# Geglu after sliding-window attention: a third seven-product quad in the last two token groups

## The chip, the cores and the metric

The kernel runs on one core of one Trainium2 chip. The metric is the device time of one execution in microseconds (us), taken as the median of several runs. TensorE does matrix products and writes them to PSUM banks, VectorE (DVE) and ScalarE (ACT) read the banks, GpSimd (POOL) works on data in on-chip memory, and SyncE (SP) issues transfers. Each engine runs its own instructions in their order; semaphores tie the engines together.

## The reference: attention, then a gated feed-forward block

For 8 batches, 8 heads, 576 positions and 64 columns a head:

```
scores = q @ k.T / 8 + slope[h] * -|i - j|        (kept where 0 <= i - j < 128)
attn   = softmax(scores) @ v
x      = attn, heads side by side                  # 4608 tokens x 512
out    = (gelu(x @ w_gate) * (x @ w_val)) @ w_out  # 512 -> 1536 -> 512
```

Inputs and the output are f32. The kernel computes the products in bf16 with f32 sums.

## The kernel before: nine token groups, quads and plain blocks

The 4608 tokens go through the feed-forward block in nine groups of 512 (g = 0 to 8). Attention of later batches runs between the groups and is finished in group 6; **groups 7 and 8 have feed-forward work alone**. The 1536 hidden columns are twelve blocks f of 128. `hid[g]` (hT in the trace) holds a group's hidden values, blocks by tokens.

Blocks are made in two ways.

A **plain block** (`gate_val`, L631) takes 8 matmuls of 512 tokens: 4 into a bank for the gate, 4 into a bank for the value. ScalarE takes the gelu of the gate (L655), VectorE multiplies (L656).

A **quad** (`gate_quad`, L811) makes four blocks at once, in a Strassen-like way: the tokens are cut in a low and a high half of 256, the inner dimension in two halves, and gate and value are the two columns of the small matrix. Seven products take the place of eight. They run in the order 1, 2, 6, 5, 7, 3, 4; each has 8 matmuls of 256 tokens, two halves u = 0 and 1 of four matmuls, each half in its own bank. Products 1, 6, 7 and 4 go into bank x of their half, 5 and 3 into y, 2 into z. So a later product accumulates on what an engine has read out in between: ScalarE copies product 1 (L849), then 1 + 6 (L855), and product 5 (L858) into three pairs of f32 staging tiles; VectorE adds banks to these (L839); ScalarE takes the gelus (L842); VectorE multiplies the low half of the tokens out of bank x (L872), GpSimd the high half out of staging (L876). In groups 6 to 8 the staging tiles are buffers of the attention part that lie idle by then (`rooms`, L805): qT0 for product 1, kT0 for 1 + 6, qT1 for product 5, and qs0 for the gelus, the same for every quad.

Products 3, 5, 6 and 7 need four sums of weights (`combine_weights`, eight instructions: four sums for two 128-row pieces), made once for a quad's place. Those for blocks 6 to 9 are in `kept`; those for blocks 0 to 3 are made by GpSimd into the tile P0 at the end of group 6. Products 4 to 7 need four sums of inputs, made by `combine_x` for each group (by VectorE for group 8, during the products of group 7).

The table `QUADS = (0, 6)` sets the order in groups 7 and 8: quad on blocks 0 to 3, plain blocks 4 and 5, quad on 6 to 9, plain blocks 10 and 11.

The **output** of groups 2 to 8 uses the same scheme (`product`, L741): the left operand is hT, split by block parity and token half; three sums of it go to `left` and one is made in place in hT (`combine_left`, L718, in four steps s1, s2, in-place a21, s4). Blocks pair up as i = 0 to 5 (blocks 2i and 2i + 1). Each product n has 6 matmuls of 256 columns for each of a = 0 and 1; groups 7 and 8 run n = 1, 2, 6, 5, 7, then 3 and 4 (group 8 begins 4 after one matmul of 3). Products 1 and 2 read the low token half of hT, 6 left sum s2, 5 s1, 7 the in-place sum, 3 s4, and 4 the high half of hT. `gather_out` names what is read out of the banks: p1, u2, p5 and c21 are copies by ScalarE, c11, c22 and c12 additions by VectorE (L902, L908, L913).

Everything is in a hand-written order: the engines execute what the program issues in its order, and nothing is rescheduled. Eight PSUM banks are shared by all of this.

Of the kernel before, what the change touches and what calls it, by code (L numbers as in the profile page):

```python
# [25 lines left out]
QUADS = (0, 6)  # L26
# [10 lines left out]
def kernel(  # L37
# [680 lines left out]
    def combine_left(g, lo, hi, which=(0, 1, 2, 3), engine=nc.vector):  # L718
        x, ns = halves(g), slice(lo, hi)
# [21 lines left out]
    def product(g, n, a, lo=0, hi=NF // 2):  # L741
        (l, r), into = FACTORS[n], INTO[n]
        first = n in (1, 2, 5)
# [4 lines left out]
        for i in range(lo, hi):  # L748
            lhsT = left[:, l, i, cols] if isinstance(l, int) else halves(g)[:, i, l[0], l[1], cols]
            rhs = right[:, r, i, :] if isinstance(r, int) else x[:, i, r[0], r[1], :]  # L750
            nc.tensor.matmul(out=made[g, a, into], lhsT=lhsT, rhs=rhs, start=first and i == 0,  # L751
                             stop=i == NF // 2 - 1, skip_group_check=True)

    def flat_of(t):
# [3 lines left out]
    sums_w = {0: [flat_of(Ps[0])[:, 1024 * n:1024 * n + 1024].rearrange("p (c f) -> p c f", c=2) for n in range(4)],  # L758
              6: [kept[:, n, :, :] for n in range(4)]}

    def combine_weights(f0, engine=nc.gpsimd):
        todo, to = [], sums_w[f0]
        for c in (0, 1):
            g1, g2, v1, v2 = (w[:, x, 128 * f0:128 * f0 + 512]
                              for w, x in ((wg, c), (wg, 2 + c), (wv, c), (wv, 2 + c)))
            s1, s2, s3, s4 = (t[:, c, :] for t in to)
# [44 lines left out]
    def gate_quad(g, f0, room=None, between=None):  # L811
# [6 lines left out]
        g1, g2, v1, v2 = (w[:, c:c + 2, 128 * f0:128 * f0 + 512] for w in (wg, wv) for c in (0, 2))  # L818
# [3 lines left out]
        def P(n):  # L822
            w, x = factors[n]
            for u in (0, 1):
# [3 lines left out]
                for e in (0, 1):  # L828
                    at = 256 * u + 128 * e
                    for c in (0, 1):  # L830
                        nc.tensor.matmul(  # L831
                            out=ps[:, 256 * e:256 * e + 256], lhsT=w[:, c, at:at + 128], rhs=x[:, c, :],
                            start=n in (1, 2, 5) and e == 0 and c == 0, stop=c == 1, skip_group_check=True)
# [10 lines left out]
        def hidden(u, half):  # L844
            return hid[g][:, f0 + 2 * u:f0 + 2 * u + 2, 256 * half:256 * half + 256]
# [24 lines left out]
        P(4)  # L870
        for u in (0, 1):
            nc.vector.tensor_tensor(out=hidden(u, 0), in0=cut(banks["x", u], 2), in1=cut(gelu_tiles[u], 2), op=ALU.mult)  # L872
            n = P5[u].shape[1]
            out, high = hidden(u, 1), cut(gelu_tiles[2 + u], n)
            if n == 2:
                nc.gpsimd.tensor_tensor(out=out, in0=P5[u], in1=high, op=ALU.mult)  # L876
            else:
                nc.gpsimd.tensor_tensor(
                    out=out.rearrange("p e (y x) -> p e y x", x=128),
                    in0=P5[u].rearrange("p (e y) x -> p e y x", e=2),  # L880
                    in1=high.rearrange("p (e y) x -> p e y x", e=2), op=ALU.mult)
# [268 lines left out]
    def out_products(g):  # L1150
# [3 lines left out]
        if b > B:  # L1154
            last = [(4, ("c21",)), (3, ("c12",))]
            for n, after in [(1, ("p1",)), (2, ()), (6, ("u2", "c11")), (5, ("p5",)), (7, ("c22",))] + (
                    last if g == NG - 1 else last[::-1]):
                early = g == NG - 1 and n in (3, 4)
                for a in (0, 1):
                    if early and a == 0 and n == 4:  # L1160
                        P(3, 0, 0, 1)
                    P(n, a, *((1,) if early and a == 0 and n == 3 else ()))
# [3 lines left out]
                if n == 6 and g + 1 < NG:  # L1166
                    combine_x(g + 1)
# [73 lines left out]
        P(3, 0, 0, 2)  # L1241
        P(4, 0)
        P(3, 0, 2)
# [39 lines left out]
    for g in range(NG):  # L1283
        if 1 <= g < B - 2:
            transposes_dma(3 if g == 1 else g + 2)
        if g >= B - 1:
            for f in range(NF):
                if f in QUADS:
                    gate_quad(g, f)
                elif not any(f0 < f < f0 + 4 for f0 in QUADS):  # L1290
                    gate_val(g, f)
                if f == 4:
                    store()
                if f == 5:
# [116 lines left out]
```

## Time and profile before

| | us |
|---|---|
| median of 3 runs (lowest to highest) | 326.07 (326.05 to 326.29) |
| the profiled execution | 324.97 |
| its span, from the first to the last instruction | 323.2 |
| group 7 from its first gate matmul to the first of group 8 (263.06 to 291.39) | 28.33 |
| group 8 to its last output matmul but the tail (291.39 to 319.72) | 28.33 |

A row of the timeline gives the start, the time of all instructions in the row, engine, line, operation, output <- inputs, shapes and count; what stands in brackets is the engine's idle time before it and what ended it. Where one row has several instructions, they overlap a little, so the start of the next is a better measure of their pace than their length. A matmul's length holds its way through the array; its pace is read from starts.

### The profile page before, as it was taken

The page shows a single profiled execution, that of the slowest core. Times are in us where ns is not written, and L with a number is a line of the kernel's source. Part 1 is how long each engine was busy: PE and PEld are TensorE (multiplying, and loading weights), DVE is VectorE, ACT ScalarE, POOL GpSimd, SP SyncE. Part 2 cuts the span into 40 slices and gives each one's busy share as a digit, 9 for nine tenths or more (in the row PEclk, how much of TensorE's full clock was granted, in tenths as well). Part 3 has the DMA queues.
Part 4 walks back from the last instruction along what each step waited for, and adds up shares of the span by engine and source line. Part 5 has one row for each costly group of instructions (what it writes and reads, how often), then busy time and mean ns, then how long its engine had stood idle before and what let it go on. Part 6 is the DMA issues. An engine that isn't in the chain of part 4 may idle for free.

```text
span 323.2 us, 9412 instructions
## 1 busy us (share of the span) xinstructions
PE 316.2 (98%) x3753; PEld 213.8 (66%) x3753; DVE 248.6 (77%) x493; ACT 219.5 (68%) x421; POOL 196.9 (61%) x228
## 2 busy tenths in 40 slices
PE   8999999999999999999989999999999999999995
PEld 4566746565554767566855786578747787788764
DVE  7789666979779877967697679877897756895692
ACT  7984678557888678657956787578767256627641
POOL 5973679385069986379936995496009496410450
PEclk9999999999999999999999999999999999999999
DMA  8999999999999979976997699759204230003003
GB/s 217 165 195 192 200 176 178 142 168 192 124 154 175 140 148 193 171 138 160 173 195 140 173 164 191 138 159 146 101 35 100 51 132 0 2 0 132 0 4 130
DMA packets 149920, 43.57 MB, mean 135 GB/s; under 512 B 133588, under 2 KB 142964, under 8 KB 149876
## 3 DMA queue, kind: packets, MB, share of 16 engines
q0 software_dynamic: 107456, 18.10, 75.6%
q1 hardware_dynamic: 41424, 23.35, 33.5%
q10 hardware_dynamic: 996, 1.53, 1.9%
q8 instruction: 29, 0.48, 0.6%
q14 instruction: 15, 0.12, 0.1%
HBM read 43.65 MB, written 9.53 MB: 165 GB/s over the span
## 4 chain that ended last, share of the span: by engine, by line
PE 91%; DMA 4%; ACT 2%; DVE 1%; issue 1%; DVEq 0%; ACTq 0%
PE ps L648 35%; PE ps L751 20%; PE ps L831 19%; PE ps L497 5%; PE ps L685 4%; DMA wo<-in_moe_w_out_dram 4%; PE ps L307 2%; PE ps L221 1%; ACT P L236 1%; PE ps L78 1%; PE ps L435 1%; PE ps L705 1%; PE ps L1001 1%; PE ps L345 1%; DVE T L391 0%
## 5 line engine op out<-in xcount | busy, mean ns | idle before, releaser
L648 PE MATMUL ps<-xT,wg 128*128 128x512 bf16 (+4 forms) x312 | 71.9, 352 | 0.0
L648 PE MATMUL ps<-xT,wv 128*128 128x512 bf16 (+4 forms) x312 | 71.8, 352 | 0.0
L655 ACT ACTIVATE gelu<-ps 128x512 bf16<-128x512 f32 (+3 forms) x77 | 41.6, 546 | 41.4 <-PE ps L648 37.6
L656 DVE TENSOR_TENSOR hT<-ps,gelu 128x512 bf16<-128x512 f32 (+3 forms) x77 | 46.3, 623 | 19.2 <-PE ps L648 15.4
L236 ACT ACTIVATE P<-ps 128x512 bf16<-128x512 f32 (+1 forms) x108 | 52.3, 578 | 5.6 <-PE ps L307 3.0
L648 PEld LDWEIGHTS <-wv 128*128 128x128 bf16 x312 | 29.2, 98 | 30.4 <-DVE xT L556 0.8
L648 PEld LDWEIGHTS <-wg 128*128 128x128 bf16 x312 | 28.7, 98 | 26.1 <-issue 0.3
L241 DVE TENSOR_TENSOR P<-P,emask 128x768 bf16<-128x768 bf16 x60 | 31.8, 551 | 7.7 <-ACT P L236 6.0
L751 PEld LDWEIGHTS <-hT 128*128 128x128 bf16 x336 | 32.1, 98 | 6.6 <-issue 0.8
L117 POOL DMA_DIRECT2D vb<-in_v_dram x40 | 34.0, 886 | 3.6 <-DMA wo<-in_moe_w_out_dram 1.0
L876 POOL TENSOR_TENSOR hT<-qT,qs 128x512 bf16<-128x512 f32 x10 | 11.5, 1166 | 26.5 <-ACT qs L842 26.5
L117 POOL DMA_DIRECT2D ks<-in_k_dram x30 | 25.4, 890 | 2.9 <-DMA qs<-in_q_dram 2.9
L751 PEld LDWEIGHTS <-left 128*128 128x128 bf16 x252 | 24.1, 98 | 4.3 <-issue 0.9
L831 PEld LDWEIGHTS <-kept 128*128 128x128 bf16 x256 | 25.0, 98 | 2.9
L117 POOL DMA_DIRECT2D qs<-in_q_dram x30 | 25.4, 863 | 1.9 <-DMA wo<-in_moe_w_out_dram 1.0
L1337 POOL COPY mark<-hT 1x2 bf16<-1x2 bf16 x5 | 0.9, 175 | 40.9 <-DVE hT L656 40.9
L751 PE MATMUL ps<-right,hT 128*128 128x256 bf16 x168 | 22.2, 273 | 0.8 <-DVE T L391 0.8
L839 DVE TENSOR_TENSOR qT<-ps,qT 128x512 f32<-128x512 f32 x20 | 12.9, 685 | 12.2 <-PE ps L831 10.9
L751 PE MATMUL ps<-right,left 128*128 128x256 bf16 x168 | 20.6, 273 | 0.8 <-issue 0.5
L751 PE MATMUL ps<-wo,hT 128*128 128x256 bf16 x168 | 21.2, 273 | 0.0
L839 DVE TENSOR_TENSOR P<-ps,P 128x512 f32<-128x512 f32 x24 | 15.1, 683 | 7.3 <-PE ps L831 7.2
L831 PE MATMUL ps<-xT,wg 128*128 128x256 bf16 x160 | 19.1, 273 | 0.0
(173 smaller groups left out, 614.5 us busy)
## 6 DMA issues: line engine op xcount, KB each, us to landing
out_dram<-osb SPq DMA_DIRECT2D x34, 256.0 KB
rb<-rd SPq DMA_DIRECT2D x8, 576.0 KB
vb<-in_v_dram POOLq DMA_DIRECT2D x32, 128.0 KB, 7.0
qs<-in_q_dram POOLq DMA_DIRECT2D x24, 128.0 KB, 6.0
ks<-in_k_dram POOLq DMA_DIRECT2D x24, 128.0 KB, 7.4
wo<-in_moe_w_out_dram POOLq DMA_DIRECT2D x4, 384.0 KB, 12.1
wg<-in_moe_w_gate_dram POOLq DMA_DIRECT2D x5, 256.0 KB, 8.4
wv<-in_moe_w_val_dram POOLq DMA_DIRECT2D x5, 256.0 KB, 9.1
```

The lines of the kernel that those rows point to most:

```text
L117: nc.gpsimd.dma_start(out=t[at:at + n, j, :].rearrange("p (h d) -> p h d", h=H), in_=src[b][:, 128 * j:128 * j + n, :].rearrange("h p d -> ...
L236: nc.scalar.activation(out=dst, in_=src, func=AF.Exp, scale=0.125)
L241: nc.vector.tensor_tensor(out=dst, in0=dst, in1=m, op=ALU.mult)
L497: mm = nc.tensor.matmul(out=out, lhsT=lhsT, rhs=prob(b)[half, c, i, col:col + q1 - q0], start=all(t[2] != u for t in todo[:n]), stop=True, ...
L648: nc.tensor.matmul(out=ps[:, a:e], lhsT=w[:, c, 128 * f:128 * (f + 1)], rhs=xT[:, c, t0 + lo + a:t0 + lo + e], start=begins and a == 0, st ...
L655: nc.scalar.activation(out=gl[:, 0:n], in_=pg, func=AF.Gelu)
L656: nc.vector.tensor_tensor(out=hid[g][:, f, lo:hi], in0=pv, in1=gl[:, 0:n], op=ALU.mult)
L685: nc.tensor.matmul(out=acc[g], lhsT=hid[g][:, f, 128 * t:128 * (t + 1)], rhs=wo[:, f, :], start=(f == 0), stop=(f == NF - 1))
L751: nc.tensor.matmul(out=made[g, a, into], lhsT=lhsT, rhs=rhs, start=first and i == 0, stop=i == NF // 2 - 1, skip_group_check=True)
L831: nc.tensor.matmul(out=ps[:, 256 * e:256 * e + 256], lhsT=w[:, c, at:at + 128], rhs=x[:, c, :], start=n in (1, 2, 5) and e == 0 and c == 0 ...
L839: nc.vector.tensor_tensor(out=to[u], in0=cut(banks[n, u], to[u].shape[1]), in1=to[u], op=ALU.add)
L876: nc.gpsimd.tensor_tensor(out=out, in0=P5[u], in1=high, op=ALU.mult)
```

## The change

`QUADS` gives way to `PAIRS`, which says for each quad which two pairs of blocks it has. A third quad takes blocks 4, 5, 10 and 11, that is, all that were plain in groups 7 and 8. It has its own sums of weights, made by GpSimd in group 7 into the tile P1, six instructions ahead of the first quad's high products and two ahead of the second's. It has its own staging tiles (kT1, vb0, vb1) and gelu tiles (qs1). Its high products are VectorE's instead of GpSimd's, after both low ones.

The output products 1, 2, 6 and 5 come in two parts: the early blocks i = 0, 1, 3, 4 of two products, then the late ones i = 2, 5. The left sums follow that: s1 and s2 of the early blocks by GpSimd, of the late ones by VectorE, the in-place sum and s4 by VectorE for all six at once. In group 8 product 4 is still begun after one matmul of product 3.

```diff
-QUADS = (0, 6)
+PAIRS = {0: (0, 2), 6: (6, 8), 4: (4, 10)}
...
-    def product(g, n, a, lo=0, hi=NF // 2):
+    def product(g, n, a, which=range(NF // 2)):
         (l, r), into = FACTORS[n], INTO[n]
-        first = n in (1, 2, 5)
+        count = made.get((g, a, n), 0)
+        first = n in (1, 2, 5) and not count
+        made[g, a, n] = count + len(which)
...
-        for i in range(lo, hi):
+        for k, i in enumerate(which):
...
...
+              4: [flat_of(Ps[1])[:, 1024 * n:1024 * n + 1024].rearrange("p (c f) -> p c f", c=2) for n in range(4)],
               6: [kept[:, n, :, :] for n in range(4)]}
+
+    def weights(w, c, f0):
+        a, b = PAIRS[f0]
+        return w[:, c, 128 * a:128 * b + 256].rearrange("p (n y) -> p n y", y=256)[:, 0:(b - a) // 2 + 1:(b - a) // 2, :]
...
-    def gate_quad(g, f0, room=None, between=None):
+    def gate_quad(g, f0, room=None, between=None, high=nc.gpsimd):
...
+        def low(u):
+            nc.vector.tensor_tensor(out=hidden(u, 0), in0=cut(banks["x", u], 2), in1=cut(gelu_tiles[u], 2), op=ALU.mult)
+
+        if high is nc.vector:
+            low(0)
+            low(1)
         for u in (0, 1):
-            nc.vector.tensor_tensor(out=hidden(u, 0), in0=cut(banks["x", u], 2), in1=cut(gelu_tiles[u], 2), op=ALU.mult)
+            if high is not nc.vector:
+                low(u)
             n = P5[u].shape[1]
-            out, high = hidden(u, 1), cut(gelu_tiles[2 + u], n)
+            out, gelus = hidden(u, 1), cut(gelu_tiles[2 + u], n)
             if n == 2:
-                nc.gpsimd.tensor_tensor(out=out, in0=P5[u], in1=high, op=ALU.mult)
+                high.tensor_tensor(out=out, in0=P5[u], in1=gelus, op=ALU.mult)
...
         if b > B:
-            last = [(4, ("c21",)), (3, ("c12",))]
-            for n, after in [(1, ("p1",)), (2, ()), (6, ("u2", "c11")), (5, ("p5",)), (7, ("c22",))] + (
-                    last if g == NG - 1 else last[::-1]):
...
+            both(1, early)
+            both(2, early)
+            both(1, late, "p1")
+            both(2, late)
+            combine_left(g, 2, 6, (0, 1), step=3)
+            both(6, early)
+            both(5, early)
+            combine_left(g, 0, 6, (3,))
+            both(6, late, "u2", "c11")
+            both(5, late, "p5")
+            combine_left(g, 0, 6, (2,))
+            if g + 1 < NG:
+                combine_x(g + 1)
+            both(7, range(NF // 2), "c22")
+            if g + 1 < NG:
+                both(3, range(NF // 2), "c12")
+                both(4, range(NF // 2), "c21")
+            else:
+                P(3, 0, range(1))
+                both(4, range(NF // 2), "c21")
+                P(3, 0, range(1, 6))
...
         if g >= B - 1:
-            for f in range(NF):
-                if f in QUADS:
-                    gate_quad(g, f)
-                elif not any(f0 < f < f0 + 4 for f0 in QUADS):
-                    gate_val(g, f)
...
-            for which in ((0, 1), (3,), (2,)):
-                for lo, hi in ((3, 5), (5, 6)) if 0 in which else ((2, 5), (5, 6)):
-                    combine_left(g, lo, hi, which)
+            sums = combine_weights(4) if g == B - 1 else []
+            for do in sums[:6]:
+                do()
+            gate_quad(g, 0)
+            store()
+            for do in sums[6:]:
+                do()
+            gate_quad(g, 6)
+            for lo, hi in ((0, 2), (3, 5)):
+                combine_left(g, lo, hi, (0, 1), engine=nc.gpsimd)
+            gate_quad(g, 4, (wide_of([(kT[1], 2), (vb[0], 2), (vb[1], 2)]), tiles_of([(qs[1], 4)])), high=nc.vector)
             out_products(g)
```

What that does to the order on the engines, at two places. Numbers of buffers are part of some names (P_105 is P0, P_106 is P1, qT_100 is qT1, qs_95 is qs0); "x2" counts equal rows. The first place is GpSimd from the end of group 6 on: the last sums of weights for blocks 0 to 3, then group 7, and the first high products of group 8. Before:

```order
L767 TENSOR_TENSOR P_105<-wg,wv 128x512 x2
L767 TENSOR_TENSOR P_105<-wg,P_105 128x512 x2
L876 TENSOR_TENSOR hT<-qT_100,qs_95 128x2x256 x2
L726 TENSOR_TENSOR left<-hT 128x512
L726 TENSOR_TENSOR left<-left,hT 128x512
L876 TENSOR_TENSOR hT<-qT_100,qs_95 128x2x256 x2
L726 TENSOR_TENSOR hT<-hT 128x2x256
L726 TENSOR_TENSOR left<-hT,left 128x512
L876 TENSOR_TENSOR hT<-qT_100,qs_95 128x2x256 x2
```

And in the changed kernel:

```order
L773 TENSOR_TENSOR P_105<-wg,wv 128x512 x2
L773 TENSOR_TENSOR P_105<-wg,P_105 128x512 x2
L773 TENSOR_TENSOR P_106<-wv 128x512 x2
L773 TENSOR_TENSOR P_106<-P_106,wg 128x512 x2
L773 TENSOR_TENSOR P_106<-wg,wv 128x512 x2
L895 TENSOR_TENSOR hT<-qT_100,qs_95 128x2x256 x2
L773 TENSOR_TENSOR P_106<-wg,P_106 128x512 x2
L895 TENSOR_TENSOR hT<-qT_100,qs_95 128x2x256 x2
L726 TENSOR_TENSOR left<-hT 128x512
L726 TENSOR_TENSOR left<-left,hT 128x512
L726 TENSOR_TENSOR left<-hT 128x512
L726 TENSOR_TENSOR left<-left,hT 128x512
```

Six sums into P1 stand between the last sums into P0 and the high products of the first quad (L895, which was L876); two more stand ahead of the second quad's, and all left sums come after both.

The second place is VectorE at the end of group 7: from what makes the last blocks of hT to the first input sum of group 8 (T). Before:

```order
L656 TENSOR_TENSOR hT<-ps,gelu 128x512 x2
L726 TENSOR_TENSOR left<-hT 128x512
L726 TENSOR_TENSOR left<-left,hT 128x512
L726 TENSOR_TENSOR left<-hT 128x256
L726 TENSOR_TENSOR left<-left,hT 128x256
L726 TENSOR_TENSOR hT<-hT 128x3x256
L726 TENSOR_TENSOR hT<-hT 128x256
L726 TENSOR_TENSOR left<-hT,left 128x768
L726 TENSOR_TENSOR left<-hT,left 128x256
L902 TENSOR_TENSOR osb<-ps,osb 128x256 x2
L789 TENSOR_TENSOR T<-xT 128x512
```

And in the changed kernel:

```order
L884 TENSOR_TENSOR hT<-ps,qs_96 128x2x256 x2
L895 TENSOR_TENSOR hT<-vb_104,qs_96 128x2x256 x2
L726 TENSOR_TENSOR left<-hT 128x2x256
L726 TENSOR_TENSOR left<-left,hT 128x2x256
L726 TENSOR_TENSOR hT<-hT 128x6x256
L921 TENSOR_TENSOR osb<-ps,osb 128x256 x2
L726 TENSOR_TENSOR left<-hT,left 128x1536
L795 TENSOR_TENSOR T<-xT 128x512
```

The two low and two high products of the third quad (L884, and L895 out of vb_104, its staging) come in where the plain blocks' products stood, the left sums are fewer and larger, and c11 (L921, which was L902) moves ahead of the last left sum.

More of the change, by code (lines that the diff above doesn't have):

```diff
@@ L1240, in out_products @@
         P(1, 1)
-        P(3, 0, 0, 2)
+        P(3, 0, range(2))
         P(4, 0)
-        P(3, 0, 2)
+        P(3, 0, range(2, 6))
         O("p1", 1)
```

52 lines of the change are left out of this document (26 added, 26 removed).

## The prediction

> **What bounds the kernel now.** I read the page first, then the list of TensorE's waits, then stretches of the last two token groups.
>
> ```profile
> PE 316.2 (98%) x3753; PEld 213.8 (66%) x3753; DVE 248.6 (77%) x493; ACT 219.5 (68%) x421; POOL 196.9 (61%) x228
> ...
> PE 91%; DMA 4%; ACT 2%; DVE 1%; issue 1%; DVEq 0%; ACTq 0%
> ```
>
> The first row is the busy time of each engine, the second the chain of work that ended last. The longest wait of TensorE:
>
> ```profile
> PE ps L78 <- DVE zeros L933: 1.0, 1, 1.0
> ```
>
> TensorE is busy for 98% of the span and makes 91% of the chain that ended last; its longest single wait is 1.0 us, at the very start. So a matmul removed is time removed, as long as no new wait appears. The stretches of groups 7 and 8 (microseconds of the span; then busy time and instructions of each engine, the granted clock, the DMA share):
>
> ```profile
> 263.06:269.18 6.12, 6.12 (x59) 5.48 (x57) 3.21 (x6) 4.54 (x9) 4.16 (x4) 1.00 0.23 86
> 269.18:272.63 3.45, 3.45 (x19) 1.56 (x16) 2.45 (x4) 2.31 (x4) 2.66 (x3) 1.00 0.00 0
> ...
> 282.19:291.39 9.20, 9.20 (x85) 8.14 (x84) 8.01 (x20) 2.60 (x7) 1.86 (x2) 1.00 0.05 19
> ...
> 310.53:319.72 9.19, 9.19 (x85) 8.04 (x83) 6.33 (x15) 3.25 (x9) 1.84 (x2) 1.00 0.14 48
> ```
>
> The rows are group 7's first quad, its first pair of plain blocks, its output products, and group 8's output products. TensorE fills every stretch without a gap, at full clock. A quad's 56 matmuls take 6.12 us, 0.109 us each; a pair of plain blocks 3.45 us. The 84 output matmuls take 9.2 us, 0.109 us each again.
>
> **The change part by part.**
>
> **Fewer columns.** Two pairs of plain blocks cost 2 × 3.45 = 6.90 us a group, a third quad 6.12. That removes 0.78 us a group, 1.56 us in both, all on the path.
>
> **Six weight sums ahead of quad 1's high products, on GpSimd.** The third quad needs its own eight sums of weights, made once, in group 7. Six of them are put into GpSimd's queue ahead of the two products that make the high half of quad 1. What GpSimd does there now:
>
> ```profile
> 262.72 2.27 POOL L767 TENSOR_TENSOR P<-wg,wv 128x512 bf16<-128x512 bf16 x2
> 264.94 2.27 POOL L767 TENSOR_TENSOR P<-wg,P 128x512 bf16<-128x512 bf16 x2
> 269.89 2.27 POOL L876 TENSOR_TENSOR hT<-qT,qs 128x512 bf16<-128x512 f32 x2 [2.67 <-ACT qs L842]
> 272.24 1.15 POOL L726 TENSOR_TENSOR left<-hT 128x512 bf16<-128x512 bf16 x1
> ```
>
> It is still on quad 1's own sums until 264.94 + 2.27 = 267.2, then idles 2.67 us, and begins the high products at 269.89, when their gelu is there. Two sums take 264.94 − 262.72 = 2.22 us, 1.11 each. Six more last until 264.94 + 2.22 + 6 × 1.11 = 273.8. The new sums read their weights in two pieces of 256; the row of L726 reads hT so, in 1.15 us, so the shape costs nothing much. The high products then end at 273.8 + 1.14 = 274.97 and 276.1, where they ended at about 271.0 and 272.16: four microseconds later.
>
> Who waits for them? They read the staging tile qT1. Quads 1 and 2 share all staging tiles, so ScalarE's copy of product 5 of quad 2 (L858, now L870) must not overwrite qT1 before. Behind that copy, product 3 accumulates into the bank that it empties. When would the copy run otherwise?
>
> ```profile
> 269.18 1.23 ACT L842 ACTIVATE qs<-kT 128x512 bf16<-128x512 f32 x2 [0.59 <-DVE kT L839]
> ...
> 272.63 1.91 PE L831 MATMUL ps<-xT,wg 128*128 128x256 bf16 x16
> ...
> 273.32 1.07 ACT L849 COPY qT<-ps 128x512 f32<-128x512 f32 x2 [0.70 <-PE ps L831]
> ...
> 275.07 1.07 ACT L855 COPY kT<-ps 128x512 f32<-128x512 f32 x2 [0.67 <-PE ps L831]
> ...
> 276.02 1.09 ACT L858 COPY qT<-ps 128x512 f32<-128x512 f32 x2
> ```
>
> In the kernel before, quad 2 starts at 272.63 and its first copy 0.69 us later. In the changed one quad 2 starts at 269.18, where the plain blocks stood. ScalarE is then still on the last two gelus of quad 1, until 270.41, so the copies of product 1 end at 270.95 and 271.48 (1.07 for two). Product 6 accumulates on what they read. It would start 16 × 0.109 us in, at 270.93, and its second half at 271.37. I take 0.17 us for these two short waits with a signal's delay; the bounds are 0 and 0.3. Product 6's copies then end at 272.8, and the copy of product 5 could start there. It has to wait for 274.97, ends with a signal's delay at 275.57, and its second half, held until 276.1, ends at 276.71.
>
> Product 3 would start at 269.18 + 40 × 0.109 + 0.17 = 273.72. Now its first half starts at 275.63 and its second at 276.77; four matmuls later, at 277.21, product 4 begins, and it ends at 278.08. Without waits quad 2 would end at 269.18 + 6.12 = 275.30. **Price: 2.78 us**, the 0.17 among it, and no work of TensorE covers it, since all later matmuls stand behind in its queue. If the copies and signals were a little quicker it is 2.6. If GpSimd's operations did not overlap by 0.04 (1.15 and 1.17 each), it is 3.1.
>
> **Quad after quad elsewhere.** The 0.17 us comes again where quad 3 follows quad 2 in group 7, and twice in group 8, where no sums precede the high products: 3 × 0.17 = 0.51, bounds 0 and 0.9. Quad 3 has staging of its own, so nothing holds its copies; ScalarE's copies and gelus of a quad (1.07 + 1.07 + 1.09 + 2 × 1.23 = 5.7 us by the rows above) still fit under its 6.12 us of matmuls. The last two weight sums end near 276.1 + 2.22 = 278.3, before quad 3's product 3, which reads them at 282.6.
>
> **VectorE at the end of a group.** The third quad ends where the output products begin. How a quad's end looks, and what VectorE's other pieces cost:
>
> ```profile
> 254.60 0.95 DVE L726 TENSOR_TENSOR hT<-hT 128x1536 bf16<-128x1536 bf16 x1
> ...
> 268.30 1.04 PE L831 MATMUL ps<-ks,wv 128*128 128x256 bf16 x8
> ...
> 269.67 1.27 DVE L872 TENSOR_TENSOR hT<-ps,qs 128x512 bf16<-128x512 f32 x2
> ...
> 286.58 0.75 DVE L902 TENSOR_TENSOR osb<-ps,osb 128x256 f32<-128x256 f32 x2
> 287.25 0.41 DVE L789 TENSOR_TENSOR T<-xT 128x512 bf16<-128x512 bf16 x1
> ...
> 288.71 0.75 DVE L908 TENSOR_TENSOR osb<-ps,osb 128x256 f32<-128x256 f32 x2
> ```
>
> The eight matmuls of a last product start at 268.30 and give way to the next work at 269.18; the low products end at 270.94, 1.76 us later. Counted from the first output matmul, VectorE therefore ends the low products at 1.76. The two high products have no row of this kind on VectorE: one input is f32 and both lie in on-chip memory. From below they are bounded by 0.42 (all bf16), from above by 0.64 (1.27 for two of L872, f32 from the matmul bank); I take 0.62, near the f32 rows, so they end at 3.0. Two left sums of 512 columns, 0.4 each as the row of L789 (same size and type), end at 3.8, the in-place one of 1536 columns (0.9, a little overlapped) at 4.65, the additions for c11 at 5.3, the last left sums, as long, at 6.2. In group 7 the four input sums of group 8 follow (288.71 − 287.25 = 1.46) until 7.65, and the first addition for c22 ends at 8.05.
>
> TensorE asks for these in the new order, each time as matmuls before it × 0.109: the late blocks of product 1 at 1.75 (low products at 1.76), of product 6 at 4.38 (left sums at 3.8), product 7 at 5.25 (4.65), product 3 at 6.56 (6.2). The two parts cover all of these. Only product 4, which accumulates into the bank that c22 reads, asks at 7.87 for what comes at 8.1. That is 0.25 us in group 7. In group 8 no input sums stand between, so c22 is read at 6.6 and product 4 starts at 6.67: nearly nothing. With product 7's short wait for its copy I take 0.3 and 0.1; the bounds are 0 and 1.2 for both.
>
> **Sum.** −1.56 + 2.78 + 0.51 + 0.4 = **+2.1 us**. Group 7 loses about 2.5, group 8 gains about 0.3. The profiled execution (324.97 us, span 323.2) would become 327.1; it lies 1.1 us under the median of the runs, 326.07, so I predict 328.2 for the median. With all low bounds it is −1.56 + 2.6 = +1.0, with all high ones −1.56 + 3.1 + 0.9 + 1.2 = +3.6: 327.1 to 329.7.
>
> **The rivals.**
>
> Not slower: GpSimd's sums hold nobody. Product 3 loses nothing if the copy of product 5 may start by 273.1, so if the six sums take under (273.1 − 1.14 − 267.16) / 6 = 0.80 us each. For it: the page calls spans on GpSimd rough, and VectorE does such a sum in 0.42. Against it: the sums of the rows above stand one behind the other at an even 1.11, in both pairs. The sum then is −1.56 + 0.17 + 0.51 + 0.4 = −0.5, 325.6; with no short wait at all it is 324.5.
>
> Slower still: VectorE and GpSimd get in each other's way.
>
> ```profile
> 279.45 2.32 POOL L876 TENSOR_TENSOR hT<-qT,qs 128x512 bf16<-128x512 f32 x2 [4.84 <-ACT qs L842]
> ...
> 280.43 0.33 DVE L726 TENSOR_TENSOR left<-hT 128x256 bf16<-128x256 bf16 x1
> ...
> 280.80 1.13 DVE L726 TENSOR_TENSOR left<-left,hT 128x256 bf16<-128x256 bf16 x1
> ```
>
> The same VectorE sum takes 0.33 us once and 1.13 us beside GpSimd's second product, until just after that ends at 281.77. In my count GpSimd ends its left sums of group 7 at 285.9: the two last weight sums at 278.3, quad 2's high products, whose gelu comes at 278.8, at 281.1, then four sums of 1.2. VectorE's high products start at 286.2. If GpSimd is half a microsecond later, one of them is held for up to 1.15 us, c22 slips by as much, and product 4 with it: 328.2 + 1.15 = 329.4. The Trainium skill (GPSIMD Engine Reference, section 8, Key points) speaks against this change here: it says that GpSimd shares its memory interfaces with VectorE and contends with VectorE instructions that have two inputs in SBUF. By that rule the high products, which have two such inputs, would be held when they overlap; the 1.13 us row agrees with it.
>
> Slower by the clock.
>
> ```profile
> 1.00 3.60 PE L78 MATMUL ps<-zeros 128*128 128x128 bf16 x11 [1.00 <-DVE zeros L933]
> ```
>
> These first 11 matmuls stream 4 × 128 + 7 × 512 = 4096 columns in about 3.5 us, 0.85 ns a column, where a quad's take 0.109 / 256 = 0.43 ns. TensorE thus starts at half pace. If the hole ahead of product 3 (1.9 us, and 0.7 after four matmuls) brought that back for as long, it would cost some 1.7 us: 329.9. No hole of this trace is longer than 1.0 us, so it cannot tell. The Trainium skill (TensorE: Matmul & The Clock Gate, Part 1) wants a whole idle window of about 3.4 us for that; by it this rival falls.
>
> **How the numbers follow.** Forecast 0.72; VectorE held 0.10; the clock 0.04; GpSimd holds nobody 0.14, which splits evenly into 325.6 or so and less. A measurement here tells about 0.2%, 0.65 us. The first three are slower: 0.86. The last gives 0.07 no change and 0.07 faster. The range 327.0 to 329.8 takes in the bounds of the sum and the held high products; outside are the last case and the clock.
>
> **What would show it.** Right: in group 7 ScalarE's L870 copies of quad 2 wait some 2 us for GpSimd's hT; TensorE's product 3 there stands 1.9 us and then 0.7; quad 2 of group 7 takes 8.9 us and that of group 8 some 6.3; group 8 ends 0.3 us sooner after its start than before. Wrong: no such wait at the copy (then the sums are quicker, or the copy is not held), or a stall of more than 0.5 us at product 4 or at the late blocks, which would mean that VectorE's chain is longer than counted.

## The result, and the profile after

The changed kernel is slower: a median of 327.86 us over ten executions against 325.52 us over ten of the kernel before, a ratio of 1.0077 (95% interval 1.0054 to 1.0101). The forecast was slower, 328.2 us. The profiled execution took 326.87 us with a span of 325.1 (before 324.97 and 323.2).

The ten executions differ in the mean clock that TensorE was granted, and the cause below needs that: three had 0.993 to 0.995 and took 328.83 us on average, seven had 0.999 or 1.000 and took 327.09.

First the page of the changed kernel: the busy times and the chain of work that ended last, by engine.

```profile
PE 312.4 (96%) x3775; PEld 218.3 (67%) x3801; DVE 252.5 (78%) x493; ACT 225.0 (69%) x433; POOL 205.5 (63%) x236
...
PE 86%; DVE 5%; issue 3%; POOL 2%; ACT 2%; DMA 1%; DVEq 0%; ACTq 0%
```

TensorE is shown busy 3.8 us less (316.2 before), and the span is 1.9 us longer. Most of the 3.8 us is no saving: this profile lacks 26 matmul records ahead of group 7 (3775 matmuls beside 3801 weight loads; 3753 and 3753 before). In groups 7 and 8 TensorE's busy time falls from 56.66 to 55.75 us, and its idle time rises from nothing to 2.52. GpSimd, which had no share in the chain before, now has 2%. Where, the stretches of groups 7 and 8 tell (time; busy time and instructions of PE, PEld, DVE, ACT and POOL; granted clock; DMA):

```profile
263.34:269.45 6.11, 6.11 (x58) 5.48 (x56) 3.20 (x6) 4.54 (x9) 6.11 (x6) 1.00 0.23 86
269.45:278.36 8.91, 6.50 (x58) 5.46 (x56) 5.05 (x9) 5.49 (x11) 8.91 (x9) 1.00 0.00 0
278.36:284.53 6.17, 6.17 (x59) 5.48 (x57) 4.95 (x9) 5.29 (x11) 5.64 (x6) 1.00 0.01 3
284.53:293.96 9.43, 9.32 (x86) 8.15 (x84) 8.96 (x19) 3.44 (x9) 1.43 (x2) 1.00 0.01 2
293.96:300.07 6.11, 6.11 (x58) 5.49 (x56) 3.20 (x6) 4.54 (x9) 0.00 (x0) 1.00 0.46 172
300.07:306.25 6.18, 6.18 (x58) 5.47 (x56) 4.95 (x9) 5.29 (x10) 2.28 (x2) 1.00 0.00 1
306.25:312.43 6.18, 6.18 (x59) 5.47 (x57) 4.98 (x9) 5.28 (x10) 5.38 (x5) 1.00 0.01 4
312.43:321.61 9.18, 9.18 (x86) 8.03 (x83) 7.40 (x14) 3.82 (x10) 1.44 (x2) 1.00 0.13 46
```

Rows one to four are group 7: three quads and the output products; rows five to eight are group 8. Group 7 takes 30.62 us (28.33 before: +2.29), group 8 27.65 (28.33: −0.68), together +1.61. The other 0.28 us of the span lies before group 7, where the two programs are the same. One row stands out: quad 2 of group 7 takes 8.91 us with TensorE busy for 6.50, and GpSimd is busy through all of it. The same quad of group 8 takes 6.18. Its rows in the timeline of the changed kernel (what stands in brackets is the idle time before a row and what ended it):

```profile
271.87 2.29 POOL L773 TENSOR_TENSOR P<-wg,wv 128x512 bf16<-128x512 bf16 x2
274.10 2.29 POOL L895 TENSOR_TENSOR hT<-qT,qs 128x512 bf16<-128x512 f32 x2
...
275.30 0.58 ACT L870 COPY qT<-ps 128x512 f32<-128x512 f32 x1 [2.32 <-POOL hT L895]
276.42 0.59 ACT L870 COPY qT<-ps 128x512 f32<-128x512 f32 x1 [0.53 <-POOL hT L895]
...
275.94 0.60 PE L842 MATMUL ps<-xT,kept 128*128 128x256 bf16 x4 [1.89 <-ACT qT L870]
277.05 0.60 PE L842 MATMUL ps<-xT,kept 128*128 128x256 bf16 x4 [0.52 <-ACT qT L870]
```

The last of the six new sums ends near 274.1; quad 1's two high products follow; each frees one half of the staging tile qT1; each of ScalarE's copies of product 5 starts right behind; each lets four matmuls of product 3 go. Behind the third quad:

```profile
286.20 1.28 DVE L895 TENSOR_TENSOR hT<-vb,qs 128x512 bf16<-128x512 f32 x2
...
292.18 0.75 DVE L927 TENSOR_TENSOR osb<-ps,osb 128x256 f32<-128x256 f32 x2
...
292.65 1.47 PE L753 MATMUL ps<-right,hT 128*128 128x256 bf16 x12
```

VectorE's two high products take 0.64 us each, nothing holds them, and product 4 starts at 292.65 where the row ahead of it would let it start at 292.39: it waits 0.26 us for the addition for c22.

### The profile page after: what moved, and what is told of

It is laid out like the page before. It is cut to its first block, busy times and chain, and to the rows that moved or that the text cites. A ratio compares the mean times of both kernels' runs of the same rounds, so it can differ in the third digit from the quotient of the medians.

```text
span 325.1 us, 9514 instructions
## 1 busy us (share of the span) xinstructions
PE 312.4 (96%) x3775; PEld 218.3 (67%) x3801; DVE 252.5 (78%) x493; ACT 225.0 (69%) x433; POOL 205.5 (63%) x236
## 4 chain that ended last, share of the span: by engine, by line
PE 86%; DVE 5%; issue 3%; POOL 2%; ACT 2%; DMA 1%; DVEq 0%; ACTq 0%
PE ps L648 32%; PE ps L842 21%; PE ps L753 17%; PE ps L497 5%; PE ps L685 4%; PE ps L307 2%; PE ps L705 2%; PE ps L221 1%; POOL P L773 1%; ACT P L236 1%; DMA wo<-in_q_dram 1%; PE ps L435 1%; POOL hT L895 1%; PE ps L159 1%; DVE qs L1003 1%
## 5 line engine op out<-in xcount | busy, mean ns | idle before, releaser
L648 PE MATMUL ps<-xT,wv 128*128 128x512 bf16 (+4 forms) x275 | 63.1, 348 | 0.2
L648 PE MATMUL ps<-xT,wg 128*128 128x512 bf16 (+4 forms) x266 | 61.3, 347 | 1.3 <-issue 0.6
L655 ACT ACTIVATE gelu<-ps 128x512 bf16<-128x512 f32 (+3 forms) x69 | 36.9, 541 | 36.4 <-PE ps L648 33.3
L656 DVE TENSOR_TENSOR hT<-ps,gelu 128x512 bf16<-128x512 f32 (+3 forms) x69 | 40.9, 616 | 16.4 <-PE ps L648 12.7
L648 PEld LDWEIGHTS <-wv 128*128 128x128 bf16 x280 | 26.2, 98 | 26.3 <-DVE xT L556 0.8
L648 PEld LDWEIGHTS <-wg 128*128 128x128 bf16 x280 | 25.6, 98 | 23.3 <-issue 0.4
L895 POOL TENSOR_TENSOR hT<-qT,qs 128x512 bf16<-128x512 f32 x10 | 11.4, 1162 | 19.1 <-ACT qs L853 19.1
L842 PE MATMUL ps<-xT,wg 128*128 128x256 bf16 x192 | 22.9, 273 | 0.0
L842 PEld LDWEIGHTS <-wg 128*128 128x128 bf16 x192 | 18.7, 98 | 3.3
```

Of the source, the lines that this page charges most:

```text
L648: nc.tensor.matmul(out=ps[:, a:e], lhsT=w[:, c, 128 * f:128 * (f + 1)], rhs=xT[:, c, t0 + lo + a:t0 + lo + e], start=begins and a == 0, st ...
L655: nc.scalar.activation(out=gl[:, 0:n], in_=pg, func=AF.Gelu)
L656: nc.vector.tensor_tensor(out=hid[g][:, f, lo:hi], in0=pv, in1=gl[:, 0:n], op=ALU.mult)
L842: nc.tensor.matmul(out=ps[:, 256 * e:256 * e + 256], lhsT=lhsT, rhs=x[:, c, :], start=n in (1, 2, 5) and e == 0 and c == 0, stop=c == 1, s ...
L895: high.tensor_tensor(out=out, in0=P5[u], in1=gelus, op=ALU.mult)
```

## The experiments

All ratios are against the kernel before, timed beside. "Group 7" is the time from its first gate matmul to that of group 8, in the profiled execution.

| kernel | median, before beside it | ratio (95%) | group 7 |
|---|---|---|---|
| e1_no_sums | 324.24, 325.45 | 0.9967 (0.9944 to 0.9990) | 27.89 |
| e3_before_sums | 325.31, 325.45 | 1.0000 (0.9978 to 1.0022) | 28.33 |
| e2_rooms | 326.45, 325.45 | 1.0027 (1.0004 to 1.0050) | 29.58 |
| e4_mend | 324.40, 325.45 | 0.9977 (0.9958 to 0.9995) | 27.94 |
| e5_four_ahead | 326.76, 325.27 | 1.0047 (1.0027 to 1.0067) | 29.56 |
| e9_eight_ahead | 331.26, 325.27 | 1.0189 (1.0164 to 1.0214) | 34.19 |
| e10_seven_ahead | 329.84, 325.06 | 1.0146 (1.0114 to 1.0179) | 32.95 |
| e6_c22_first | 327.86, 325.06 | 1.0091 (1.0056 to 1.0126) | 31.98 |
| e7_high_pool | 328.52, 325.27 | 1.0121 (1.0090 to 1.0153) | 31.39 |
| e8_one_part | 330.81, 325.27 | 1.0162 (1.0127 to 1.0198) | 33.20 |

**Without the sums.** The eight sums are left out and the third quad reads those of blocks 6 to 9.

```diff
-              4: [flat_of(Ps[1])[:, 1024 * n:1024 * n + 1024]...
+              4: [kept[:, n, :, :] for n in range(4)],
...
-            sums = combine_weights(4) if g == B - 1 else []
+            sums = []
```

> The changed kernel without the third quad's eight weight sums: its products read the sums kept for blocks 6 to 9 instead, so the values of blocks 4, 5, 10 and 11 are not the reference's; every other instruction stays. Theory (the six sums delay the first quad's high products on GpSimd, ScalarE's copy of product 5 waits for them, product 3 for the copy): the copy no longer waits, quad 2 of group 7 takes 6.2 us instead of 8.9, group 7 27.9 instead of 30.6; against the kernel before 27.9 + 27.65 - 56.66 = -1.1 us, ratio about 0.9966. Rival A (three quads in a row, or VectorE's longer chain, cost the time wherever the sums are): quad 2 of group 7 keeps some 2 us of waits, and the kernel stays 1 us or more slower than before. Rival C (runs of the changed kernel are slow for another reason, such as the clock): the trace's group 7 is short, but the timed runs stay near +2 us.

As expected: quad 2 of group 7 takes 6.17 us, no copy and no product 3 waits, and the kernel is faster than before.

```profile
269.68:275.85 6.17, 6.17 (x58) 5.46 (x56) 4.94 (x9) 5.29 (x10) 2.28 (x2) 1.00 0.00 0
```

**The sums alone.** The kernel before, with six sums of the same size (of blocks 4 to 7) at the same place in GpSimd's queue and nobody who reads them.

```diff
+              4: [flat_of(Ps[1])[:, 1024 * n:1024 * n + 1024].rearrange("p (c f) -> p c f", c=2) for n in range(4)],
...
+            if g == B - 1:
+                for do in combine_weights(4)[:6]:
+                    do()
```

> The kernel before with the six weight sums of the third quad added at the same place of GpSimd's queue in group 7, their results unused. Theory: with two plain blocks between the quads the second quad's copy of product 5 comes at 276.0, and the first quad's high products end near 275.0 and 276.1, so nobody waits: 0.0 us, within 0.2. GpSimd's left sums of blocks 0 to 3 move from 272.2 to about 276.1, which nobody reads before the output products. Rival A (the sums cost time by themselves, through the memory interface or through the order of GpSimd): +1 us or more.

```profile
263.36:291.69 28.33, 28.33 (x230) 1.00 0.07 25
```

TensorE fills group 7 to the last hundredth (the row has its busy time alone, 28.33 of 28.33, behind it clock and DMA). Quad 1's high products start at 274.14 here, as late as in the changed kernel, and hold nobody, since the first plain pair still stands between the quads. So the price lies neither in the sums nor in the quad, but in both at once: the change delays the high products by 4 us and takes out the 3.45 us of plain blocks that would have covered it.

**Other tiles.** Quads 2 and 3 exchange their staging, so that quad 2 doesn't need what quad 1's high products still read.

```diff
-            gate_quad(g, 6)
+            other = (wide_of([(kT[1], 2), (vb[0], 2), (vb[1], 2)]), tiles_of([(qs[1], 4)]))
+            gate_quad(g, 6, other)
...
-            gate_quad(g, 4, (wide_of([(kT[1], 2), ...]), tiles_of([(qs[1], 4)])), high=nc.vector)
+            gate_quad(g, 4, high=nc.vector)
```

> The changed kernel with the staging and gelu tiles of quads 2 and 3 exchanged: quad 2 of each group works in kT1, vb0, vb1 and qs1, quad 3 in the tiles of quad 1. GpSimd's queue is as in the changed kernel. Theory: the copy of product 5 of quad 2 has nobody to wait for, and quad 2 of group 7 takes 6.2 us. GpSimd's left sums still end near 285.6 us of the span, while the output products now begin near 281.8 and ask for the sums of i = 3 at 281.8 + 2.8 = 284.6: a new wait of about 1.1 us at product 6. Group 7 about 28.8 us against 28.33 before and 30.6, group 8 27.65; in all -0.2 us against the kernel before, between -0.6 and +0.4. Rival A (not the staging tile): quad 2 of group 7 stays at 8.9 us and the kernel at +2. Rival B (GpSimd's queue does not matter once the tile is free): no wait at product 6, -1.1 us.

Quad 2 falls to 6.18 us with GpSimd's queue as before, which shows that the hold is that of the shared tile. But the kernel is 1.0 us slower than before where −0.6 to +0.4 was expected. Its timeline behind the third quad:

```profile
283.66 2.97 DVE L895 TENSOR_TENSOR hT<-qT,qs 128x512 bf16<-128x512 f32 x2
...
284.60 1.48 POOL L726 TENSOR_TENSOR left<-left,hT 128x512 bf16<-128x512 bf16 x1
...
286.14 2.58 PE L753 MATMUL ps<-right,left 128*128 128x256 bf16 x22 [1.16 <-POOL left L726]
...
291.80 1.36 PE L753 MATMUL ps<-right,hT 128*128 128x256 bf16 x11 [0.31 <-DVE osb L927]
```

With the stall gone TensorE is 2.7 us further on, and GpSimd's left sums, which the stall had given time, are late: product 6 waits 1.16 us. VectorE's high products now run beside them and take 2.97 us for two instead of 1.28, and GpSimd's last sum 1.48 instead of 1.16. That is the rival "VectorE and GpSimd get in each other's way", in a kernel where the two meet: 1.69 us more for the two products, where the rival had up to 1.15 for one of them. TensorE sees less of it: the longer sum is 0.32 of product 6's 1.16 us, and product 4 waits 0.31. VectorE's two low products, which read one input from a PSUM bank, take 1.28 us beside the same sums (282.47 to 283.75), as they do in the changed kernel.

**Both late pieces mended.** Exchanged tiles, the last two sums (s4) by VectorE between quads 2 and 3, and group 8's input sums behind the addition for c22.

```diff
+            both(7, range(NF // 2), "c22")
             if g + 1 < NG:
                 combine_x(g + 1)
-            both(7, range(NF // 2), "c22")
...
             store()
-            for do in sums[6:]:
-                do()
-            gate_quad(g, 6)
+            gate_quad(g, 6, (wide_of([(kT[1], 2), (vb[0], 2), (vb[1], 2)]), tiles_of([(qs[1], 4)])))
+            if sums:
+                for do in combine_weights(4, nc.vector)[6:]:
+                    do()
...
-            gate_quad(g, 4, (wide_of([(kT[1], 2), ...]), tiles_of([(qs[1], 4)])), high=nc.vector)
+            gate_quad(g, 4, high=nc.vector)
```

> The changed kernel with three edits: the tiles of quads 2 and 3 exchanged; the last two weight sums by VectorE between quads 2 and 3 instead of by GpSimd; in group 7 the input sums of group 8 after the additions for c22 instead of ahead of them. Theory: no wait is left but the short ones of 0.06 us between quads; GpSimd ends its left sums near 283.3 us, before product 6 asks at 284.6; product 4 of group 7 doesn't wait. Groups 7 and 8 take 27.65 us each: -1.36 us against the kernel before, ratio about 0.9958; between -0.8 and -1.5. Rival: VectorE's two sums are held by GpSimd (0.33 us once, 1.13 beside GpSimd in the kernel before) and push the third quad's additions back, product 4 of quad 3 waits, and less than 0.8 us is gained.

Faster than the kernel before, by 1.05 us in the medians.

```profile
264.48:292.42 27.94, 27.94 (x255) 1.00 0.06 20
292.42:320.07 27.65, 27.65 (x254) 1.00 0.15 54
```

No wait of TensorE is listed in either group. By these rows it saves 0.39 + 0.68 = 1.07 us of the 1.56 that the columns are worth. Group 8 takes the 27.65 us expected; group 7 takes 0.29 us more, of which 0.18 lies in the third quad (6.36 us) and 0.11 in the output products (9.29). VectorE's two sums take 1.81 us there, beside GpSimd's high products (2.47 in place of 2.28), so the hold that the rival named is there. That it makes the 0.29 us was not shown apart, and the gain stays above the rival's 0.8.

**How many sums stand ahead: four, eight, seven.** The changed kernel has six. The edit for four; with seven, 7 stands in its place, and with eight all sums stand ahead.

```diff
-            for do in sums[:6]:
+            for do in sums[:4]:
...
-            for do in sums[6:]:
+            for do in sums[4:]:
```

> As the changed kernel, but only four of the six weight sums stand ahead of quad 1's high products in group 7; the other four stand between quad 1 and quad 2. Theory of the prediction (the place in GpSimd's queue sets the hold): the first high product of quad 1 ends near 273.1 and frees its staging half in time, the second near 274.1, so product 3 of quad 2 stands only 0.3 to 0.6 us before its second half, and quad 2 of group 7 takes 6.5 to 6.8 us in place of 8.91. GpSimd's left sums then end about as late as in the kernel with exchanged tiles, so product 6 of the output waits up to 1.2 us for them. Sum: +0.2 to +1.0 us against the kernel before (ratio 1.0006 to 1.003). Rival (the amount of GpSimd work in group 7 costs, wherever it stands, or the cost is the clock's): it stays at the changed kernel's +1.6 to +2.5 us (ratio 1.005 to 1.008).

> As the changed kernel, but all eight weight sums stand ahead of quad 1's high products in group 7. Theory: two more sums of 1.11 us move both high products by 2.2 us, so the hold of product 3 grows from 1.9 to 4.1 us and quad 2 of group 7 takes 11.1 us; the same GpSimd work follows, so nothing else changes: +2.2 us on the changed kernel, +3.8 to +4.5 us against the kernel before (ratio 1.012 to 1.014), and the granted clock stays at 1.0. Rival (clock): the hole is now longer than 3.4 us; if TensorE falls to half pace after such a hole, the matmuls behind it take 0.218 us in place of 0.109 for some 3.4 us, the quad takes about 12.8 us, the granted clock in the row reads below 1, and the total is +5.5 to +6.2 us (ratio 1.017 to 1.019). The second rival (amount of GpSimd work): no more than the changed kernel, +1.6 to +2.5 us.

> As the changed kernel, but seven weight sums stand ahead of quad 1's high products in group 7, between the six of the change and the eight of the run before. The hold is to be 1.89 + 1.11 = 3.0 us, then 0.5 us after four matmuls. Both theories of the clock give +1.1 us by the hold itself, so executions at full clock take +2.7 to +3.2 us against the kernel before. Theory A (the clock falls only after a window of about 3.4 us in which TensorE does nothing at all): a hole of 3.0 us holds no such window, so no execution has a mean clock below 0.997 more often than the kernel before has. Theory B (the clock falls after a window of about 3.4 us that lies at any phase and in which TensorE is busy for less than some 0.4 of it; 0.4 is an estimate, from half pace in 8 of 22 executions with holes of 1.89 and 0.51 us and in 5 of 5 with 4.11 and 0.52): about eight executions in ten have a mean clock of 0.995 and take 1.7 us more, +4.4 to +4.9 us against the kernel before, and the median lies there (ratio 1.0135 to 1.015).

The waits of product 3 in the timelines, first with four sums ahead:

```profile
276.20 0.60 PE L842 MATMUL ps<-xT,kept 128*128 128x256 bf16 x4 [0.35 <-ACT qT L870]
```

With seven ahead:

```profile
278.29 0.77 PE L842 MATMUL ps<-xT,kept 128*128 128x256 bf16 x4 [3.04 <-ACT qT L870]
```

With eight ahead:

```profile
278.85 0.60 PE L842 MATMUL ps<-xT,kept 128*128 128x256 bf16 x4 [4.11 <-ACT qT L870]
```

1.89 us with six sums, 3.04 with seven, 4.11 with eight: 1.1 us a sum, GpSimd's pace. With four only the second half of product 3 waits, 0.35 us, and quad 2 takes 6.68. The hold is set by the place in GpSimd's queue, as the prediction had it. Four ahead is not what was expected in the total, though (+0.2 to +1.0). Its trace gives +1.23 for group 7 (product 6 waits 0.62 us for the left sums) and −0.68 for group 8, so +0.55, but the medians differ by 1.5 us. Two of its twelve executions had a clock of 0.995 and 0.997, which does not make up for 0.9 us. With eight and seven ahead the medians exceed what the two groups show by 0.8 as well (+5.2 and +3.9 by the trace). In these three profiles group 7 begins at 264.0 to 264.7, in most others at 263.1 to 263.6, though the program ahead of it is the same; but in e4_mend, whose median shows no such excess, it begins at 264.48 too. Why is open.

Eight ahead cost 6.0 us, where the hold alone would make 3.8 to 4.5. Quad 2 takes 12.32 us there, 1.2 more than its waits explain. All five executions had a mean clock of 0.995. Two stretches of 3.41 us each of the profiled one, TensorE alone, then the granted clock:

```profile
276.08:279.49 3.41, 0.60 (x4) 1.00 0.00 0
279.49:282.90 3.41, 2.94 (x14) 0.50 0.02 5
```

Behind the hole the clock is granted at one half for 3.41 us, and then in full again. That is the rival that had been given 0.04. With seven ahead the hole is 3.04 us and holds no 3.4 us without work; still five of six executions had 0.993 to 0.995, and the median came out at +4.8 us, in the range of theory B (+4.4 to +4.9), not of A (+2.7 to +3.2). The number of executions tells the two apart better than the median, since 0.8 of the 4.8 us is the open part above. The stretches of the profiled one:

```profile
275.17:278.58 3.41, 0.38 (x4) 1.00 0.00 0
278.58:281.99 3.41, 3.06 (x16) 0.50 0.02 5
```

**c22 ahead of the input sums.**

```diff
+            both(7, range(NF // 2), "c22")
             if g + 1 < NG:
                 combine_x(g + 1)
-            both(7, range(NF // 2), "c22")
```

> As the changed kernel, but in group 7 the four input sums of group 8 stand behind the first addition for c22 on VectorE, not ahead of it. Theory (they make c22 late for product 4): the addition is done some 1.4 us sooner, product 4 no longer stands 0.26 us, output products of group 7 take 9.17 in place of 9.43 us, and group 8's first use of the sums, 2.4 us into its first quad, is not held. -0.26 us on the changed kernel, about +1.4 us against the kernel before in an execution at full clock; the half pace after the hole of quad 2 comes in as many executions as in the changed kernel (about a third, mean clock near 0.995). Rival (c22 is not late by the input sums but by the left sums ahead): the wait at product 4 stays at 0.2 to 0.3 us.

```profile
292.41 1.47 PE L753 MATMUL ps<-wo,left 128*128 128x256 bf16 x12
293.72 1.47 PE L753 MATMUL ps<-right,hT 128*128 128x256 bf16 x12
```

Product 4 follows product 3 after 1.31 us, the 12 matmuls of that product, without a wait; the output products take 9.17 us. So the 0.26 us were the input sums' doing. The median doesn't show it, since four of its six executions (a third was expected) had a clock of 0.993 to 0.995, the profiled one too. That one has the very hole of the changed kernel (1.91 us, four matmuls, 0.52 us), and shows what the changed kernel's own profile, taken in an execution at full clock, could not:

```profile
273.57:276.98 3.41, 0.99 (x8) 1.00 0.00 0
276.98:280.39 3.41, 3.41 (x18) 0.50 0.02 5
```

The stretch behind the hole in the changed kernel's own profile:

```profile
277.01:280.42 3.41, 3.37 (x31) 1.00 0.02 5
```

18 matmuls run in 3.41 us at half clock, 31 at full clock. Quads 2 and 3 together take 16.70 us in e6_c22_first and 15.08 in the changed kernel's profile, with the same holes: the half clock costs 1.62 us. In the stretch before the fall, TensorE had been busy for 0.99 us of 3.41.

**High products on GpSimd again.**

```diff
-            gate_quad(g, 4, (wide_of([(kT[1], 2), ...]), tiles_of([(qs[1], 4)])), high=nc.vector)
+            gate_quad(g, 4, (wide_of([(kT[1], 2), ...]), tiles_of([(qs[1], 4)])))
```

> As the changed kernel, but GpSimd makes the high half of the third quad as it does for the others. Theory (VectorE's chain behind the quad sets product 4): in group 7 GpSimd's left sums end at 286.04, so its two high products end near 288.3 where VectorE's end at 287.5; the left sums of blocks 2 and 5, the in-place sum, c11, the last left sum, the input sums and the first addition for c22 all slip by 0.8 us, and product 4 with them; the late blocks of product 6 wait up to 0.4 us of it. Group 7 takes 31.2 to 31.7 us in place of 30.62. In group 8, where GpSimd is free by then, the high products end as early as VectorE's: no change, 27.65. Sum: +0.5 to +1.1 us on the changed kernel, +2.1 to +3.4 us against the kernel before (ratio 1.006 to 1.0105). Rival (who makes the high half does not matter, TensorE's order covers it): no change to the changed kernel.

Group 7 takes 31.39 us, as expected: product 6 waits 0.18 us, product 4 0.31 and a little lies between. The median is 3.25 us over the kernel before, within the +2.1 to +3.4. Group 8 was expected unchanged and is 0.76 us longer.

```profile
285.81 2.27 POOL L895 TENSOR_TENSOR hT<-vb,qs 128x512 bf16<-128x512 f32 x2
...
314.48 2.27 POOL L895 TENSOR_TENSOR hT<-vb,qs 128x512 bf16<-128x512 f32 x2
...
317.73 1.05 PE L753 MATMUL ps<-right,left 128*128 128x256 bf16 x8 [0.17 <-DVE left L726]
```

In group 8, too, GpSimd is not free when the gelus are there: its left sums last until 314.48, so its high products end at 316.75, 3.7 us behind the third quad (313.02), where VectorE's end 3.0 behind it in the changed kernel. That VectorE makes the third quad's high half is worth 0.8 us in each group.

**The output products in one part.**

```diff
-            both(1, early)
-            both(2, early)
-            both(1, late, "p1")
-            both(2, late)
+            both(1, range(NF // 2), "p1")
+            both(2, range(NF // 2))
```

Products 6 and 5 likewise.

> As the changed kernel, but output products 1, 2, 6 and 5 are each made in one part again, all six blocks in order. Theory (TensorE reaches block 2 of product 1 some 0.2 us after the third quad, VectorE has the low half of that block only 1.1 us after it and of block 5 after 1.76): product 1 stops for about 0.9 us ahead of block 2 and for about 0.4 us ahead of block 5, in both groups; all later requests come 1.3 us later and find their data, so that product 4's wait of 0.26 in group 7 goes. Sum: +2.2 to +2.6 us on the changed kernel, +3.8 to +4.9 us against the kernel before (ratio 1.012 to 1.015). Rival (the order of the output products does not matter): no change to the changed kernel.

```profile
287.27 2.85 PE L753 MATMUL ps<-wo,hT 128*128 128x256 bf16 x22 [0.83 <-DVE hT L884]
...
316.20 2.85 PE L753 MATMUL ps<-wo,hT 128*128 128x256 bf16 x22 [0.84 <-DVE hT L884]
```

Product 1 stops 0.83 us after two matmuls in both groups, and the 22 behind it take 0.3 us more than their pace, which fits the short wait expected ahead of block 5. The output products of group 7 take 10.45 us in place of 9.43, those of group 8 1.27 more than in the changed kernel: +2.3, as expected. The medians differ by 5.5 us from the kernel before, beyond the +3.8 to +4.9. Three of six executions had a clock of 0.989 to 0.993, the profiled one too; the two with 1.000 took 328.6 and 329.56, +3.3 and +4.3. The sixth, with 0.998, took 331.17, which the clock does not explain.

## Why the prediction was right, and where it was not

**Fewer columns, −0.78 a group.** Right: the first quad takes 6.11 us against 6.90 for two plain pairs.

**Six sums ahead of quad 1's high products, +2.78.** Right in place, cause and size. Quad 2 of group 7 takes 8.91 us against the 8.90 counted; the copies wait 2.32 and 0.53 us, product 3 1.89 and 0.52. Leaving out the sums, giving quad 2 another tile, or keeping the plain blocks as cover each removes it, and a seventh and an eighth sum add 1.1 us each.

**Quad after quad, +0.51.** Right in kind, too large: quads that follow a quad take 6.17 to 6.18 us, 0.06 more than 6.11, not 0.17.

**VectorE behind the third quad, +0.3 and +0.1.** The chain was counted well: the high products 0.6 us each, product 4 0.26 us late in group 7 (0.25 counted), by the input sums. The output products take 9.43 us there, 0.23 more than before, and 9.18 in group 8, no more than before, so the 0.1 was not there.

With the measured sizes the sum is −1.56 + 2.79 + 3 × 0.06 + 0.23 = +1.6, not +2.1; groups 7 and 8 together show +1.61, and the executions at full clock +1.6 in the median (327.14 against 325.52).

**"By it this rival falls": the step that failed.** The rival of the clock got 0.04, on the ground that no 3.4 us pass without work. Three of the ten executions of the changed kernel had a mean clock of 0.993 to 0.995 and took 1.74 us more on average than the other seven, close to half of 3.41 us, the rival's 1.7. Half clock for 3.41 of 327 us makes a mean of 0.995; a lower mean need not cost more (in the profile of e8_one_part, 0.991, the clock is also at one half for the last 2.2 us, in which no matmul is left). In e6, e7 and e8 the executions with 0.995 or less took 1.3 to 1.8 us more than the others. These are small groups, but the traces give 1.62 for the same thing. In its own profile the clock stayed at 1.00; that the hole of quad 2 is the place is read from the profile of e6_c22_first, with the same hole (that of e8_one_part shows the fall there too). Over the four kernels with this hole 12 of 28 executions had 0.995 or less; with a hole of 3.04 us 5 of 6, with 4.11 us 5 of 5; of the kernel before 2 of 63 timed beside the experiments, of the three kernels without any such hole (e1, e3, e4) none of 36, and of the two with holes of up to 1.2 us (e2, e5) one of 24. The rival should have been a term: about 0.4 × 1.7 = 0.7 us. (The prediction took the half pace at the start from the pace of the first 11 matmuls. The clock column reads 1.00 in that stretch, so the column alone would not have shown it; behind the holes pace and column agree.) The Trainium skill (TensorE: Matmul & The Clock Gate, Part 1) says that the window is free-running, and this agrees: the same hole costs in some executions and not in others. Its wording that an idle window of about 3.4 us is needed does not agree when read as a window without work: in the stretches ahead of the fall TensorE was busy for 0.99 and 0.38 of 3.41 us. Its length of the window, about 3.4 us, agrees with the 3.41 us at half clock.

**The level.** 328.2 rested on the 326.07 of three runs. Ten of the kernel before have 325.52, 35 others 325.45: about 0.55 us lower. So 327.86 is 0.5 us less by the short waits, 0.55 less by the level and 0.7 more by the clock. That the median came within 0.4 us of the forecast is in part luck: errors that cancel.

**The rivals.** GpSimd's sums hold somebody: the sums follow each other at 1.11 us in the changed kernel as well (271.87 to 274.10 for two). VectorE and GpSimd do not meet in the changed kernel: GpSimd's last left sum ends at 286.04, VectorE's high products start at 286.20, 0.16 us apart. Without the stall they meet (e2_rooms), and the Trainium skill (GPSIMD Engine Reference, section 8, Key points), which says that the two contend where VectorE has two inputs in SBUF, agrees with the 2.97 us there. The prediction's own pair of rows was a weaker sign than it says: the sum of 0.33 us (280.43 to 280.76) also lies beside GpSimd's products (279.45 to 281.77), so not every such sum is held. A plainer pair in the kernel before are two sums of 512 columns: 1.26 us at 283.07, beside GpSimd's sum from 282.90 to 284.05, and 0.42 at 284.37, after it.

## What to carry to other kernels

When an edit puts work ahead in one engine's queue and takes work out of another's, cost the two together: follow what stands behind it to the tile that it frees and to the product that waits for that tile, and ask what covered the delay before. A stall also gives the other engines time; when you remove it, look for what was only just in time, as the left sums were. And price a hole of TensorE by more than its length: here the matmuls behind a hole of 1.9 us ran at half pace for 3.41 us in some executions and not in others, though TensorE had done some work in the 3.41 us before. How little work is too little was not measured.

## What was not expected of the hardware

- TensorE's clock fell to one half for 3.41 us after stretches of 3.41 us in which it was busy for 0.99 us, or 0.38. With a hole of 1.9 us, four matmuls and 0.5 us the mean clock was 0.995 or less in 12 of 28 executions, with one of 3.0 us in 5 of 6.
- VectorE and GpSimd slow each other, not only the one the other: two products of 512 columns took VectorE 2.97 us in place of 1.28, and GpSimd's sum beside them 1.48 in place of 1.16 (e2_rooms; in e5_four_ahead 2.45 and 1.48). VectorE's low products of the same size, with one input from a PSUM bank, took 1.28 beside GpSimd's sums as well.
